# Attention with softmax exponentials shared by ScalarE and VectorE: five shifted readings instead of six, key tiles shared out by the plan, more buffers

## The chip, the cores and the metric

The kernel runs on one core of a Trainium2 chip: TensorE (PE in the profile's rows, its weight loads PEld), VectorE (DVE), ScalarE (ACT), GpSimd (POOL) and SyncE (SP, which issues transfers). The metric is the device time of one execution in microseconds (us), the median of several runs. A traced execution has a span, from its first to its last instruction, and a time of its own a little above it.

## The reference

One transformer block over 2048 tokens of width 512, with 32 heads of 16, conditioned by a vector `c`:

```python
mod = (_silu(c) @ w_mod).reshape(c.shape[0], 6, 1, -1)
h = _layernorm(x) * (1 + ca) + sa
# _A_ref: 32 heads, Dh = 16
scores = jnp.einsum('bhqd,bhkd->bhqk', q, k) * Dh ** (-0.5)
p = _softmax(scores, axis=-1)
o = jnp.einsum('bhqk,bhkd->bhqd', p, v)
x = x + ga * _A_ref(h, A_wqkv, A_wo)
h = _layernorm(x) * (1 + cb) + sb
x = x + gb * _B_ref(h, B_w1, B_b1, B_w2, B_b2)   # 512 -> 1376 -> 512, gelu
```

The exponentials are 32 x 2048 x 2048 = 134 million values, and they carry the time.

## The kernel before

**Runs and tiles.** Queries go in four blocks of 512. A run is one block with four heads at a time; there are 32 runs (0 to 31), eight to a block. (The last block's runs hold eight heads and half the queries.) Within a run the keys go in 16 tiles of 128. A key tile has two halves, each of two heads: one QK matmul pair per half (line 675) writes a PSUM tile `st` of 128x1024 scores, of which there are three.

**Two ways to the exponential.** A tile of ScalarE (kind `qkA`) takes one activation per half (`exp_a`, line 697) into a buffer `pt`, of which there are `NPT` = 7. Then one value matmul group (`pv_op`, line 754, four matmuls) multiplies both halves with the values `VEB` and adds to the run's accumulator `od`. A tile of VectorE (kind `qkD`) takes two additions (`exp_d`, line 712) that turn the scores into 16-bit integers in a buffer `ph` (two of these), whose bits read as bf16 are a piecewise linear exponential. That reading is coarse, so it is averaged with shifted ones: for each further reading j, one VectorE addition of `PH_SH[j]` over 128x2048 integers (line 723) writes a tile `sh`, and one more value matmul group multiplies it with values `VX` that carry a weight `PH_W[j]`. With `NPH` = 6 readings such a tile costs VectorE 2 + 5 instructions and TensorE six value groups. The weighted values `VX` are made once by GpSimd (line 620).

**The accumulator is one PSUM bank.** There is a single `od`. At the end of a run VectorE copies it out (`normalise`, line 782), and only then can the next run's first value group start. Until then the next run's exponentials pile up in `pt`.

**Who takes which tile.** Key tiles 2, 6, 10 and 14 (`DKS`) can go to VectorE. A table `PAT` fixes how many of them do in each run: none in run 0, three in runs 1 to 4, three or four afterwards. The lists `a_list` and `d_list` hold the tiles in order.

**What sets the order.** A planner (`Plan`) simulates the engines with fixed durations while the program is written out. It picks the next instruction of each engine by start time and a priority (`dyn`), and that order is what each engine then runs, in order, on the chip. QK matmuls for VectorE are gated: a run's tile is not begun ahead of ScalarE's run (after run 4, at most one run ahead). All other TensorE work (projections, the output product, the two layers of the feed-forward part, in `block_tail`) carries due times: these count ScalarE exponentials done (`n_a[1]`), with steps such as `APR`, `TAIL` and `CB`. `TAIL` spreads a block's output and feed-forward work over the runs of the next block. Where TensorE would idle, the planner inserts dummy matmuls on `warm` (into `od`, line 760, or `ax`, line 352).

**After the last run,** `last_half` computes the output of the last 256 queries: it needs `od` of run 31 (line 970, a shuffle, then reciprocals at line 979).

Of the kernel before, what the change touches and what calls it, by code (L numbers as in the profile page):

```python
# [16 lines left out]
I16 = mybir.dt.int16  # L17
# [4 lines left out]

NPH = 6
PH_SH = [round(128 * j / NPH) for j in range(NPH)]


# [193 lines left out]
def kernel(  # L222
# [15 lines left out]
    P = 128  # L238
    S = 2048
    D = 512  # L240
    F = 1376
    NC = D // P
    NT = S // P
    QB = 512
# [6 lines left out]
    QSC = 0.25 * 128.0 / math.log(2.0)  # L251
    ESC = math.log(2.0) / 128.0
    DKS = (2, 6, 10, 14)
    NPT = 7
    FEW = 2
    MM = 512 / 2400.0
    PAT = [0] + [3] * 4 + [4] * 3 + [3, 4, 3, 4, 4, 4, 4, 4] * 3

    psum = bass.MemoryType.PSUM
    const = ctx.enter_context(tc.tile_pool(name="const", bufs=1))  # L260
# [7 lines left out]
    def res(name, n, shape, dt, pool=work):  # L268
        return Res(name, n, lambda i: pool.tile(shape, dt, name=f"{name}{i}"))
# [2 lines left out]
    r_od = res("od", 1, [P, QB], FP32, pp)  # L272
    r_ax = res("ax", 1, [P, QB], FP32, pp)
    r_pt = res("pt", NPT, [P, 2 * QB], BF16)
    r_ph = res("ph", 2, [P, 4 * QB], I16)
    r_sh = res("sh", 4, [P, 4 * QB], I16)
    r_xb = res("xb", 2, [P, TPB, D], BF16)
    r_blk = res("blk", NQ, [P, NC, D], BF16)
# [15 lines left out]
    n_a = [0, 0]  # L294
    n_d = [0, 0]
    urgent = set()
    aux_at = [0.0]

    def dyn(plan, o):
        if o.eng != "PE":  # L300
            return o.prio
        same = -0.5 if o.mode[0] == plan.mode else 0.0
        if o.kind == "qkA":
            back = n_a[0] - n_a[1]
            return (0.0 if back == 0 else 2.2 if back == 1 else 6.0) + same
        if o.kind == "qkD":
            back = n_d[0] - n_d[1]
            return (1.0 if back == 0 else 7.0) + same
        if o.kind == "pv":
            few = sum(f <= plan.now + 0.3 for f in r_pt.free) <= FEW  # L310
            return (0.2 if few else 3.0) + same
        if o.kind in urgent:
            return 0.5 + same
        if o.due <= n_a[1]:
            return 2.5 + same
        return (4.0 if plan.now >= aux_at[0] else 8.0) + same

    def later(o):
        return o.kind not in ("qkA", "qkD", "pv", "last", "heat") and o.kind not in urgent and o.due > n_a[1]

    APR = 26
    TAIL, CB = 150, 40
    TAIL2, TAIL3 = 120, 90
    plan = Plan(dyn, later)
    plan.need = lambda: plan.free["ACT"] + 0.92 * (n_a[0] - n_a[1])
    due_now = [1e9, 0.0]
# [8 lines left out]
    def due(at, step=0.0):  # L335
        due_now[:] = [at, step]
# [12 lines left out]
    def heat():  # L349
        if o_warm.end is None or plan.now > plan.until:  # L350
# [29 lines left out]
    VX = {(t, ph): keep.tile([P, 32 * VW + 15], BF16, name=f"VX{t}_{ph}")  # L380
          for t in DKS for ph in range(1, NPH)}
    kT = [[keep.tile([P, QB], BF16, name=f"kT{cc}_{b}") for b in range(NQ)] for cc in range(NC)]
# [212 lines left out]
    def make_v(b, cc, kind, acq, eng):  # L595
# [16 lines left out]
        for t in DKS:  # L612
            if t // TPB == b:
# [4 lines left out]
                def scale(o, t=t, vf=vf):  # L618
                    for ph in range(1, NPH):
                        nc.gpsimd.tensor_scalar(  # L620
# [11 lines left out]
    NR = len(runs)  # L632
    LAST = NQ - 1
# [3 lines left out]
        b, u = runs[r]  # L637
        return (u % NC, None, u // NC) if b == LAST else (u // 2, u % 2, None)

    def dks(r):  # L640
        return DKS[:PAT[r]]
    a_list = []
    d_list = []
    for r in range(NR):
        dk = dks(r)
        a_list += [(r, kt, h) for kt in range(NT) if kt not in dk for h in range(2)]
        d_list += [(r, kt, h) for kt in dk for h in range(2)]
    o_e = {}
    left = [0] * NR
    begun = [False] * NR  # L650
# [1 line left out]
    o_last = [None] * NR  # L652
    o_OT = {}
    a_run = [0]
    made = {"A": 0, "D": 0}
    pv_left = {}

    def qk_op(which, n):
        r, kt, half = (a_list if which == "A" else d_list)[n]
        b = runs[r][0]  # L660
        cc, par, hb = run_heads(r)
        kb, ko = divmod(kt, TPB)
        qm, evs = o_q[(cc, b)]

        def go(o):
            (n_a if which == "A" else n_d)[0] += 1
            q_left[(cc, b)] -= 1
            if q_left[(cc, b)] == 0:
                qm.uses -= 1
            if which == "A":  # L670
                a_run[0] = r
            for g in range(2):
                i = 2 * half + g
                rows = slice(32 * i, 32 * i + 32)
                nc.tensor.matmul(out=o.tile[:, g * QB:(g + 1) * QB],  # L675
                                 lhsT=kT[cc][kb][rows, ko * P:(ko + 1) * P],
                                 rhs=qm.tile[rows, par, :] if hb is None else
                                 qm.tile[rows, :, hb * HB:(hb + 1) * HB], start=True, stop=True)
            nxt(which)
        if which == "D" and half == 0:  # L680
            o_ph[0] = op("POOL", None, 0.0, (), lat=0.0, prio=0.0, acq=r_ph)
        o = op("PE", go, MM, ([o_ph[0]] if which == "D" else []) + [evs[par or 0]] + [o_k[(cc, kb)]], lat=PEL, mode=("qk", half),
               kind="qk" + which, acq=r_st, rel=(qm,),
               gate=(lambda: n_a[0] - n_a[1] < 2) if which == "A" else
               (lambda: n_d[0] - n_d[1] < 2 and r <= a_run[0] + (r > 4)))
        (exp_a if which == "A" else exp_d)(o, r, kt, half)

    def nxt(which):
        made[which] += 1
        todo.append(which)  # L690

    todo = []

    def exp_a(qk, r, kt, half):
        def go(o):
# [77 lines left out]
        plan.add(o)  # L773

    for r in range(NR):
        left[r] = NT + len(dks(r)) * (NPH - 1)
    ended = []


# [112 lines left out]

    def block_tail(b, nt=TPB):
        kind = "tail"
        due(n_a[1] + 12, (TAIL if b < LAST - 1 else TAIL2 if b < LAST else TAIL3) / (9 * nt - 1))
        N = nt * P
        xr = load_x(b)
        x2 = xr
# [3 lines left out]
        for t in range(nt):  # L902
# [11 lines left out]
        h, hd, za, trs = layer_norm(lambda t: x2.tile[:, t, :], res_done, modB, o_late["mB"],  # L914
                                    None, r_blk, ("DVE",) * 4, r_ax, kind, 1.6, None, nt)
# [123 lines left out]
    for b in range(NQ):  # L1039
        kind = f"in{b}"  # L1040
        if b < 2:
            urgent.add(kind)
        o_h[b], o_hd[b], za, trs = layer_norm(
            lambda t, b=b: o_x[b].tile[:, t, :], o_x0 if b == 0 else [o_x[b]] * TPB, modA, o_mA, prev_tr, r_blk,
# [18 lines left out]
    q_made = [0]  # L1063

    def first_run(g):
        return 2 * g if g < LAST * NC else LAST * 8 + g - LAST * NC

    def want_q(g):
        while q_made[0] < g and q_made[0] + 1 < NQ * NC:
            q_made[0] += 1  # L1070
            b, cc = divmod(q_made[0], NC)
            due(32 + APR * (first_run(q_made[0]) - 1) - 26)
            make_q(b, cc, f"q{q_made[0]}", r_ax)
            due(1e9)
            if cc == NC - 1:
                o_h[b].uses -= 1
                if b == NQ - 1:
                    o_w[0].uses -= 1

    state = {"late": 0}  # L1080
    qk_op("A", 0)
    want_q(1)
    qk_op("D", 0)
    while True:
        if not plan.step():
            break
        while todo:
            which = todo.pop(0)
            n = made[which]
            lst = a_list if which == "A" else d_list  # L1090
            if n < len(lst):
                r = lst[n][0]
                want_q(r // 2 + 1 if r < LAST * 8 else r - LAST * 4 + 2)
                qk_op(which, n)
        while ended:
            r = ended.pop(0)
            if r < NR - 1:
                normalise(r)
            b, u = runs[r]
            for cc in range(1, NC):  # L1100
                if r >= 2 * cc - 3:
                    urgent.add(f"c{cc}")
                    urgent.add(f"in{cc}")
            urgent.add("in3")
            for g in range(NQ * NC):
                if first_run(g) <= r + 2:
                    urgent.add(f"q{g}")
            if r == 0:
                late_loads(o_last[0])
                o_late["ga"] = gate_bc(ga_bc, o_late[2], "gate")  # L1110
                lt = {3: o_late[3], 4: o_late[4]}
                gt = o_late["g"]

                class V:
                    pass
                va, vb = V(), V()
                o_late["mB"] = None
                state["gt"] = gt
# [53 lines left out]
```

## Time and profile before

| | us |
|---|---|
| median of 3 runs | 890.87 |
| lowest and highest | 885.26, 892.78 |
| the profiled execution's own time | 886.78 |
| its span | 884.9 |
| POOL busy in the span | 102.5 |

The profiled execution is 4.1 us (0.5%) under the median and 1.9 us above its own span. In the profile's rows, `x` stands for a count, busy time is a union of intervals, and a wait names the instruction that waited, then what released it. A tile's number tells one use of a buffer from another.

### The profile page before, as it was taken

Reading aid. Unit: us, or ns where it says so; the run is one execution under the profiler, and the core shown is the slowest. Engines: PE = TensorE matmul, PEld = TensorE weight load, DVE = VectorE, ACT = ScalarE, POOL = GpSimd, SP = SyncE. Lnnn points to the kernel's source line nnn. Section 1 sums busy time; section 2 is a strip of 40 time slices with the busy share of each in tenths; the row PEclk is TensorE's granted clock in tenths of the full one; section 3 lists DMA queues with packets and bytes.
Section 4 is the critical chain, followed back from the end, with each engine's and each line's share of the span. In section 5 each row is a group of like instructions: output and inputs, shape, how many; then the busy total and the mean of one; then the engine's idle time right before and its main releaser. Section 6 shows DMA issues by size and latency. Waiting matters only on the chain.

```text
span 884.9 us, 20946 instructions
## 1 busy us (share of the span) xinstructions
PE 799.5 (90%) x8725; PEld 305.0 (34%) x8806; DVE 806.6 (91%) x1178; ACT 784.4 (89%) x834; POOL 102.5 (12%) x231
## 2 busy tenths in 40 slices
PE   8889999898899998999998898898889998999887
PEld 3433333332233332232222332232244443444433
DVE  7748889799999999999899999999999998989993
ACT  3799999999899998998899799999989699998752
POOL 4531312200001100000001000000002000000010
PEclk9999999999999999999899999999999998999999
DMA  6204001011000000000100000000100000000000
GB/s 191 96 12 108 14 14 39 14 35 35 32 15 14 14 14 14 21 27 8 37 14 13 14 15 14 8 26 20 37 16 15 16 12 29 26 21 21 10 31 24
DMA packets 31625, 25.13 MB, mean 28 GB/s; under 512 B 13773, under 2 KB 26926, under 8 KB 31530
## 3 DMA queue, kind: packets, MB, share of 16 engines
q1 hardware_dynamic: 31002, 23.78, 9.2%
q8 instruction: 69, 1.13, 0.5%
q14 instruction: 26, 0.21, 0.1%
q10 hardware_dynamic: 528, 0.00, 0.0%
HBM read 21.16 MB, written 2.61 MB: 27 GB/s over the span
## 4 chain that ended last, share of the span: by engine, by line
DVE 40%; PE 27%; ACT 24%; issue 8%; POOL 1%; DMA 0%; POOLq 0%; ACTq 0%; DVEq 0%
DVE ln_s L485 2%; PE od_8878 L754 1%; PE od_12701 L754 1%; PE od_5765 L754 1%; PE od_3837 L754 1%; PE od_12171 L754 1%; ACT g_4820 L928 1%; DVE g_7884 L925 1%; PE od_8082 L754 0%; PE ax_12106 L890 0%; PE od_13281 L754 0%; PE od_9269 L754 0%; DVE OD_14324 L979 0%; PE od_11607 L754 0%; PE od_6173 L754 0%
## 5 line engine op out<-in xcount | busy, mean ns | idle before, releaser
L754 PEld LDWEIGHTS <-VEB_89 128*32 128x32 bf16 x640 | 16.8, 98 | 19.9 <-issue 15.3
L754 PEld LDWEIGHTS <-VEB_91 128*32 128x32 bf16 x640 | 16.8, 96 | 15.7 <-issue 12.7
L754 PEld LDWEIGHTS <-VEB_92 128*32 128x32 bf16 x640 | 16.0, 96 | 14.3 <-issue 11.8
L754 PEld LDWEIGHTS <-VEB_90 128*32 128x32 bf16 x640 | 15.9, 96 | 14.4 <-issue 10.9
L921 PEld LDWEIGHTS <-W_83 128*128 128x128 bf16 x176 | 13.9, 97 | 19.5 <-issue 11.5
L675 PEld LDWEIGHTS <-kT_0_113 32*128 32x128 bf16 x128 | 6.5, 91 | 21.4 <-issue 19.2
L675 PEld LDWEIGHTS <-kT_0_117 32*128 32x128 bf16 x128 | 6.9, 91 | 20.4 <-issue 19.6
L675 PEld LDWEIGHTS <-kT_0_121 32*128 32x128 bf16 x128 | 6.8, 91 | 19.5 <-issue 19.0
L675 PEld LDWEIGHTS <-kT_3_124 32*128 32x128 bf16 x128 | 7.0, 91 | 17.4 <-issue 16.8
L675 PEld LDWEIGHTS <-kT_1_114 32*128 32x128 bf16 x128 | 6.4, 92 | 18.9 <-issue 16.3
L675 PEld LDWEIGHTS <-kT_2_115 32*128 32x128 bf16 x128 | 7.0, 91 | 17.1 <-issue 15.1
L675 PEld LDWEIGHTS <-kT_2_127 32*128 32x128 bf16 x128 | 6.7, 91 | 17.7 <-issue 17.0
L675 PEld LDWEIGHTS <-kT_1_126 32*128 32x128 bf16 x128 | 6.0, 91 | 19.3 <-issue 18.5
L675 PEld LDWEIGHTS <-kT_1_118 32*128 32x128 bf16 x128 | 6.8, 91 | 16.8 <-issue 16.2
L675 PEld LDWEIGHTS <-kT_0_125 32*128 32x128 bf16 x128 | 7.0, 91 | 16.0 <-issue 15.3
L501 ACT ACTIVATE blk_14329<-ax_14416,modB 128x256 bf16<-128x256 bf16 x2 | 1.0, 561 | 13.0 <-PE ax_14416 L1002 13.0
L675 PEld LDWEIGHTS <-kT_1_122 32*128 32x128 bf16 x128 | 5.9, 91 | 18.7 <-issue 18.5
L675 PEld LDWEIGHTS <-kT_3_116 32*128 32x128 bf16 x128 | 6.2, 91 | 17.3 <-issue 15.9
L675 PEld LDWEIGHTS <-kT_2_123 32*128 32x128 bf16 x128 | 6.3, 91 | 16.3 <-issue 15.8
L675 PEld LDWEIGHTS <-kT_2_119 32*128 32x128 bf16 x128 | 6.2, 91 | 16.1 <-issue 15.8
L675 PEld LDWEIGHTS <-kT_3_128 32*128 32x128 bf16 x128 | 5.8, 91 | 17.0 <-issue 16.8
L675 PEld LDWEIGHTS <-kT_3_120 32*128 32x128 bf16 x128 | 5.9, 91 | 16.5 <-issue 15.9
(5047 smaller groups left out, 3274.9 us busy)
## 6 DMA issues: line engine op xcount, KB each, us to landing
W_83<-in_B_w_dram SPq DMA_DIRECT2D x1, 1376.0 KB
g_1026<-in_w_mod_dram SPq DMA_DIRECT2D x2, 512.0 KB
xb_131<-in_A_x_dram SPq DMA_DIRECT2D x4, 128.0 KB
blk_181<-in_w_mod_dram SPq DMA_DIRECT2D x1, 512.0 KB
blk_185<-in_w_mod_dram SPq DMA_DIRECT2D x1, 512.0 KB
w_210<-in_A_wqkv_dram SPq DMA_DIRECT2D x1, 512.0 KB
w_214<-in_A_wqkv_dram SPq DMA_DIRECT2D x1, 512.0 KB
xb_219<-in_A_x_dram SPq DMA_DIRECT2D x1, 512.0 KB
```

Source lines behind the costliest of these rows:

```text
L485: nc.vector.bn_stats(out=st6, in_=src)
L501: nc.scalar.activation(out=dst, in_=src, func=ACT.Identity, bias=mod[:, j:j + 1], scale=mod[:, NC + j:NC + j + 1])
L675: nc.tensor.matmul(out=o.tile[:, g * QB:(g + 1) * QB], lhsT=kT[cc][kb][rows, ko * P:(ko + 1) * P], rhs=qm.tile[rows, par, :] if hb is None ...
L754: nc.tensor.matmul(out=o_od[r].tile[32 * i:32 * i + 32, n * HB:n * HB + w], lhsT=v_tile(kt, ph)[:, c0:c0 + 32], rhs=got[i // 2][:, at:at + ...
L921: nc.tensor.matmul(out=o.tile[:, 0:N], lhsT=W1[:, j, f * P:(f + 1) * P], rhs=h.tile[:, j, 0:N], start=(j == 0), stop=(j == NC - 1))
L925: ev.append(op("DVE", lambda o, f=f, mm=mm: nc.vector.tensor_scalar(out=g.tile[:, f, 0:N], in0=mm.tile[:, 0:N], scalar1=b1c[:, f:f + 1], s ...
L928: ge = op("ACT", lambda o: nc.scalar.activation(out=g.tile[:, :, 0:N], in_=g.tile[:, :, 0:N], func=ACT.Gelu_apprx_tanh), 0.1 + 1.2 * nt + ...
```

## The change

Five readings instead of six (`NPH`); three `ph` buffers instead of two; nine `pt` buffers instead of seven. The table `PAT` is gone. ScalarE owns the tiles outside `DKS` (and all of run 0); tiles in `DKS` are shared, and each engine asks `next_tile` for work when its last QK matmul has been placed. VectorE takes the first shared tile of the run that `d_run` names: a run ahead of ScalarE's, or ScalarE's own, where at least 6 us (`D_TIME`) of ScalarE work are left in it by the plan. ScalarE takes a shared tile when a run's own tiles are used up. VectorE's next tile is placed when a `ph` buffer is free within 1 us of the plan's time and the run is ScalarE's or (after run 3) the next. Due times count both engines' halves, 32 a run, with the steps raised in proportion.

```diff
-NPH = 6
+NPH = 5
...
-    NPT = 7
+    NPT = 9
...
-    PAT = [0] + [3] * 4 + [4] * 3 + [3, 4, 3, 4, 4, 4, 4, 4] * 3
+    FIRST_D, D_TIME = 1, 6.0
...
-    r_ph = res("ph", 2, [P, 4 * QB], I16)
+    r_ph = res("ph", 3, [P, 4 * QB], I16)
...
-        if o.due <= n_a[1]:
+        if o.due <= n_a[1] + n_d[1]:
...
-    APR = 26
-    TAIL, CB = 150, 40
-    TAIL2, TAIL3 = 120, 90
+    APR = 32
+    TAIL, CB = 185, 49
+    TAIL2, TAIL3 = 148, 110
...
+    own = [[kt for kt in range(NT) if r < FIRST_D or kt not in DKS] for r in range(NR)]
+    shared = [[kt for kt in DKS if r >= FIRST_D] for r in range(NR)]
+    at = {"A": [0, 0, 1], "D": [0, 0, 1]}
...
+    def d_run():
+        for r in range(max(at["D"][0], a_run[0]), NR):
+            if shared[r] and (r > a_run[0] or D_TIME < 0.92 * (
+                    2 * (len(own[r]) + len(shared[r]) - 1) + n_a[0] - n_a[1])):
+                return r
+        return NR
...
+            if which == "A" and own[r]:
+                return r, own[r].pop(0), 0
+            if which == "A" and shared[r]:
+                left[r] -= NPH - 1
+                return r, shared[r].pop(), 0
+            if which == "D" and shared[r] and r >= d_run():
+                return r, shared[r].pop(0), 0
...
-               (lambda: n_d[0] - n_d[1] < 2 and r <= a_run[0] + (r > 4)))
+               (lambda: n_d[0] - n_d[1] < 2))
...
-        due(n_a[1] + 12, (TAIL if b < LAST - 1 else TAIL2 if b < LAST else TAIL3) / (9 * nt - 1))
+        due(n_a[1] + n_d[1] + 15, (TAIL if b < LAST - 1 else TAIL2 if b < LAST else TAIL3) / (9 * nt - 1))
...
+        if not live["A"]:
+            qk_op("A")
+        if not live["D"] and (at["D"][2] == 0 or (min(r_ph.free) <= plan.now + 1.0
+                                                  and d_run() <= a_run[0] + (a_run[0] > 3))):
+            qk_op("D")
```

Counted over the two programs' instructions:

| engine, kind | before | after |
|---|---|---|
| DVE scores to integers (712 before, 733 after) | 228 | 246 |
| DVE shifts (723, 744) | 570 | 492 |
| ACT exponentials (697, 718) | 796 | 778 |
| PE value matmuls on `sh` | 2880 | 2480 |
| PE value matmuls on `pt` and `ph` | 2560 | 2560 |
| PE dummy matmuls into `od` (760, 781) | 156 | 176 |
| POOL values `VX` weighted, and their memsets | 80, 40 | 64, 32 |
| SP | 168 | 168 |

So VectorE takes 123 tiles instead of 114, of 124 that may be shared: runs 1 to 4 have four instead of three, run 5 has three, every later run four.

VectorE at the end of run 25, where block 2's output and feed-forward work (`blk`, `g`) runs between the attention of block 3. `od_10524` is run 25's accumulator before; `sh` rows are shifts, `ph` of two numbers are two tiles. Before:

```order
L723 TENSOR_SCALAR sh_11029<-ph_10795 128x2048
L712 TENSOR_SCALAR ph_10983<-st_11021 128x1024
L504 TENSOR_SCALAR blk_10663<-ax_11031,modB 128x512
L723 TENSOR_SCALAR sh_11059<-ph_10795 128x2048
L723 TENSOR_SCALAR sh_11066<-ph_10795 128x2048
L504 TENSOR_SCALAR blk_10663<-ax_11061,modB 128x512
L723 TENSOR_SCALAR sh_11089<-ph_10795 128x2048
L723 TENSOR_SCALAR sh_11097<-ph_10983 128x2048
L586 TENSOR_TENSOR qm_10271<-ax_11091,qmask 128x1024
L782 COPY OD_11112<-od_10524 128x512
```

The run's last tile (`ph_10795`) still has four shifts to go, and a shift of the next tile and a query mask stand before the copy. After, the same place, with `od_10186` the accumulator:

```order
L744 TENSOR_SCALAR sh_10686<-ph_10328 128x2048
L733 TENSOR_SCALAR ph_10643<-st_10683 128x1024
L504 TENSOR_SCALAR blk_10356<-ax_10688,modB 128x512
L744 TENSOR_SCALAR sh_10716<-ph_10328 128x2048
L744 TENSOR_SCALAR sh_10723<-ph_10328 128x2048
L504 TENSOR_SCALAR blk_10356<-ax_10718,modB 128x512
L744 TENSOR_SCALAR sh_10750<-ph_10500 128x2048
L803 COPY OD_10758<-od_10186 128x512
```

The last tile has three shifts there, the query mask has gone ahead, and the integers of two later tiles (`ph_10500`, `ph_10643`) are already made.

VectorE at the end of run 31, the last. Before, in front of the shuffle that starts the last stage:

```order
L723 TENSOR_SCALAR sh_14224<-ph_14005 128x2048
L925 TENSOR_SCALAR g_13501<-ax_14219,b1c 128x256
L723 TENSOR_SCALAR sh_14251<-ph_14005 128x2048
L723 TENSOR_SCALAR sh_14253<-ph_14147 128x2048
L723 TENSOR_SCALAR sh_14263<-ph_14147 128x2048
L723 TENSOR_SCALAR sh_14273<-ph_14147 128x2048
L723 TENSOR_SCALAR sh_14288<-ph_14147 128x2048
L925 TENSOR_SCALAR g_13501<-ax_14283,b1c 128x256
L723 TENSOR_SCALAR sh_14307<-ph_14147 128x2048
L925 TENSOR_SCALAR g_13501<-ax_14309,b1c 128x256
```

All these come behind the last exponential's scores, and the run's last value group is that of `sh_14307`. After:

```order
L744 TENSOR_SCALAR sh_13616<-ph_13427 128x2048
L744 TENSOR_SCALAR sh_13626<-ph_13427 128x2048
L744 TENSOR_SCALAR sh_13644<-ph_13427 128x2048
L744 TENSOR_SCALAR sh_13659<-ph_13427 128x2048
L946 TENSOR_SCALAR g_13067<-ax_13692,b1c 128x256
L946 TENSOR_SCALAR g_13067<-ax_13724,b1c 128x256
```

The last shift now stands ahead of the last scores, and the run's last value group is that of ScalarE's last tile.

More of the change, by code (lines that the diff above doesn't have):

```diff
@@ L318, in later @@
     def later(o):
-        return o.kind not in ("qkA", "qkD", "pv", "last", "heat") and o.kind not in urgent and o.due > n_a[1]
-    APR = 26
-    TAIL, CB = 150, 40
-    TAIL2, TAIL3 = 120, 90
+        return o.kind not in ("qkA", "qkD", "pv", "last", "heat") and o.kind not in urgent and o.due > n_a[1] + n_d[1]
+    APR = 32
+    TAIL, CB = 185, 49
+    TAIL2, TAIL3 = 148, 110
     plan = Plan(dyn, later)
@@ L638, in run_heads @@
         return (u % NC, None, u // NC) if b == LAST else (u // 2, u % 2, None)
[L640 to L647, printed above, removed]
+    own = [[kt for kt in range(NT) if r < FIRST_D or kt not in DKS] for r in range(NR)]
+    shared = [[kt for kt in DKS if r >= FIRST_D] for r in range(NR)]
+    at = {"A": [0, 0, 1], "D": [0, 0, 1]}
     o_e = {}
@@ L654, with next_tile, qk_op @@
     a_run = [0]
-    made = {"A": 0, "D": 0}
     pv_left = {}
-    def qk_op(which, n):
-        r, kt, half = (a_list if which == "A" else d_list)[n]
+    def d_run():
[4 more added lines that the diff above has]
+        return NR
+    def next_tile(which):
+        r, kt, half = at[which]
+        if half == 0:
+            return r, kt, 1
+        while r < NR:
+            if which == "A" and own[r]:
[5 more added lines that the diff above has]
+                return r, shared[r].pop(0), 0
+            r += 1
+        return None
+    def qk_op(which):
+        got = next_tile(which)
+        if got is None:
+            return
+        at[which][:] = got
+        r, kt, half = got
+        want_q(r // 2 + 1 if r < LAST * 8 else r - LAST * 4 + 2)
+        live[which] += 1
         b = runs[r][0]
@@ L678, in go @@
                                  qm.tile[rows, :, hb * HB:(hb + 1) * HB], start=True, stop=True)
-            nxt(which)
+            live[which] -= 1
         if which == "D" and half == 0:
@@ L684, in qk_op @@
                gate=(lambda: n_a[0] - n_a[1] < 2) if which == "A" else
-               (lambda: n_d[0] - n_d[1] < 2 and r <= a_run[0] + (r > 4)))
+               (lambda: n_d[0] - n_d[1] < 2))
         (exp_a if which == "A" else exp_d)(o, r, kt, half)
[L688 to L692, printed above, removed]
+    live = {"A": 0, "D": 0}
     def exp_a(qk, r, kt, half):
@@ L775 @@
     for r in range(NR):
-        left[r] = NT + len(dks(r)) * (NPH - 1)
+        left[r] = NT + len(shared[r]) * (NPH - 1)
     ended = []
@@ L1071, in want_q @@
             b, cc = divmod(q_made[0], NC)
-            due(32 + APR * (first_run(q_made[0]) - 1) - 26)
+            due(32 + APR * (first_run(q_made[0]) - 1) - 32)
             make_q(b, cc, f"q{q_made[0]}", r_ax)
@@ L1080 @@
     state = {"late": 0}
-    qk_op("A", 0)
+    qk_op("A")
     want_q(1)
-    qk_op("D", 0)
     while True:
+        if not live["A"]:
+            qk_op("A")
+        if not live["D"] and (at["D"][2] == 0 or (min(r_ph.free) <= plan.now + 1.0
+                                                  and d_run() <= a_run[0] + (a_run[0] > 3))):
+            qk_op("D")
         if not plan.step():
             break
[L1087 to L1094, printed above, removed]
         while ended:
```

## The prediction

> **What bounds the kernel now.** I read the busy shares first, then the same by stage, then what each engine waited for, and last the end of the chain. The profile's first part:
>
> ```profile
> span 884.9 us, 20946 instructions
> PE 799.5 (90%) x8725; PEld 305.0 (34%) x8806; DVE 806.6 (91%) x1178; ACT 784.4 (89%) x834; POOL 102.5 (12%) x231
> ```
>
> Three engines are at 90%, so no single one carries the time. By stage (the stretch's length, then busy time of each engine, then the granted clock):
>
> ```profile
> 75.00:200.00 125.00, 115.28 (x1179) 42.87 (x1189) 107.61 (x160) 121.99 (x133) 23.65 (x41) 0.97 0.10 28
> 200.00:850.00 650.00, 593.21 (x6822) 220.54 (x6883) 626.78 (x880) 600.25 (x628) 44.84 (x39) 0.98 0.07 19
> 75.00:850.00 775.00, 708.48 (x7997) 263.41 (x8072) 734.38 (x1039) 722.24 (x759) 68.49 (x80) 0.98 0.07 21
> ```
>
> From 75 to 850 us runs 1 to 31 go on; DVE is busy 734.4 of 775 us (94.8%), ACT 722.2 (93.2%), PE 708.5 (91.4%). From 200 us on DVE is at 96.4%: it is the fullest, and ACT has 49.8 us idle there. What ends ACT's idle time in that stretch, longest first:
>
> ```profile
> ACT pt_11151 L697 <- PE od_11122 L754: 6.3, 1, 6.3
> ACT pt_7743 L697 <- PE od_7730 L754: 5.1, 1, 5.1
> ACT pt_13883 L697 <- PE od_13854 L754: 4.8, 1, 4.8
> ACT pt_13314 L697 <- PE od_13281 L754: 4.2, 1, 4.2
> ACT pt_3854 L697 <- PE od_3837 L754: 2.8, 1, 2.8
> ACT pt_6580 L697 <- PE od_6563 L754: 2.5, 1, 2.5
> ACT pt_6954 L697 <- PE od_6941 L754: 2.4, 1, 2.4
> ACT pt_10081 L697 <- PE od_10051 L754: 2.4, 1, 2.4
> ACT pt_8500 L697 <- PE od_8487 L754: 2.0, 1, 2.0
> ACT pt_5387 L697 <- PE od_5374 L754: 1.8, 1, 1.8
> ...
> ACT pt_2254 L697 <- PE st_2245 L675: 1.1, 1, 1.1
> ```
>
> Ten waits make 34.3 us of ACT's 52.8 us idle. Each is for a value matmul into a new accumulator, that is, the end of a run. The longest, in order of time on ACT and DVE:
>
> ```profile
> 690.54 1.04 ACT L697 ACTIVATE pt_11050<-st_11047 128x1024 bf16<-128x1024 f32 x1
> 697.88 1.02 ACT L697 ACTIVATE pt_11151<-st_11053 128x1024 bf16<-128x1024 f32 x1 [6.30 <-PE od_11122 L754]
> ...
> 692.67 0.70 DVE L723 TENSOR_SCALAR sh_11089<-ph_10795 128x2048 int16<-128x2048 int16 x1
> ...
> 696.06 0.68 DVE L782 COPY OD_11112<-od_10524 128x512 f32<-128x512 f32 x1
> ```
>
> DVE is late with the last shift of run 25 (693.4 us); the accumulator is copied at 696.1, the next run's first value matmul follows, frees a `pt` buffer, and ACT goes on at 697.9. All seven `pt` buffers held exponentials of run 26 until then. So I counted, in the program's order before, how many of the next run's ScalarE scores stand on PE ahead of a run's last value group. It is seven or more (as many as there are buffers) at the ends of runs 7, 11, 14, 15, 17, 19, 23, 25, 29 and 30, and these are exactly the ten waits above; at all other ends it is six or fewer. That is the rule I use below.
>
> **The change, part by part.** Durations are from these sums over a line (busy time, count) and the table loads among the first:
>
> ```profile
> 0.00:890.00 890.00, 746.84 (x799) 0.98 0.10 28
> ...
> 0.00:890.00 890.00, 278.06 (x228) 0.98 0.10 28
> ...
> 0.00:890.00 890.00, 377.87 (x570) 0.98 0.10 28
> ...
> 0.00:890.00 890.00, 341.65 (x5440) 126.27 (x5440) 0.98 0.10 28
> ...
> L697 ACT ACT_TABLE_LOAD x3 | 3.8, 1283 | 0.1
> ```
>
> In this order they are the exponentials (line 697), the integers (712), the shifts (723) and the value matmuls (754). An exponential is (746.8 - 3.8) / 796 = 0.933 us, an integer half 278.06 / 228 = 1.220, a shift 377.87 / 570 = 0.663, a value matmul 341.65 / 5440 = 0.063.
>
> *VectorE.* A tile costs 2 x 1.220 + 5 x 0.663 = 5.75 us before and 5.09 with four shifts. 114 x 5.75 = 655.9 becomes 123 x 5.09 = 626.2: 29.7 us less, or 734.4 - 29.7 = 704.7 us from 75 us on. Runs 1 to 5 get 19 tiles instead of 16, so DVE gains 4.7 us of work there, where it has 17.4 idle; the relief, 34.4 us, is all in runs 6 to 31.
>
> *ScalarE.* Nine tiles fewer are 18 exponentials: 18 x 0.933 = 16.8 us off an engine that is on the path at both ends of every run. This comes off the end: **-16.8**.
>
> *TensorE.* 400 value matmuls fewer x 0.063 = 25 us; 20 dummies more give some 2 back. PE's 708.5 goes to about 685. It is not the fullest engine before or after, so this is counted at nothing; the work of ACT and DVE covers it. Were PE the bound instead, its 23 us would come off in place of the terms here, and the time would be 864.
>
> *The run ends.* Two more `pt` buffers let ACT run two exponentials further, and the shorter tail of shifts, with integers made up to three tiles ahead, brings the copy earlier. By the same count, now against nine buffers, nine or more stand ahead only at the ends of runs 4 and 25 (eleven each), 10 and 18 (nine each); elsewhere it is eight or fewer. Four waits of the present mean, 34.3 / 10 = 3.4 us, instead of ten: **-20.6**. The bounds are 0 (every end waits as long as now for another reason) and -34.3 (none waits). I take the count, since it named all ten of the present waits and no other.
>
> *The last run.* Its end before:
>
> ```profile
> 847.71 1.03 ACT L697 ACTIVATE pt_14217<-st_14198 128x1024 bf16<-128x1024 f32 x1
> ...
> 852.73 0.68 DVE L723 TENSOR_SCALAR sh_14307<-ph_14147 128x2048 int16<-128x2048 int16 x1
> ...
> 853.47 0.40 PE L754 MATMUL od_13854<-sh_14307,VX_5_112 128*32 128x256 bf16 x8
> ...
> 854.02 0.74 DVE L970 STREAM_SHUFFLE OD_14324<-od_13854 128x512 f32<-128x512 f32 x1
> ```
>
> The last stage starts 6.3 us behind the last exponential, since DVE still shifts. After, the last shift stands ahead of the last scores, so the shuffle follows an exponential (1.0), a value group (0.4) and the step to DVE (0.1 to 0.8): about 2.3 us. **-4.0**, between 0 and -4.4.
>
> *What is given back.* These three would leave 775 - 16.8 - 20.6 = 737.6 us for 704.7 us of DVE work, 95.5% against 94.8% now. A queue that waits less for one partner waits for another, so I hold DVE to the share that it has now over the whole stretch: 704.7 / 0.948 = 743.3, **+5.7**. The bounds are 0 and, if nothing of the run ends is gained, +20.6.
>
> *At nothing.* `VX` weights and memsets on GpSimd (24 instructions fewer, engine 12% busy, early); the buffers' memory; SP's queue, which is not moved. Due times go from 24 to 26 halves a run to 32, and the steps with them (`TAIL` 150 to 185), so the projections and the feed-forward part stay where they were within a fifth of a run.
>
> **Sum.** -16.8 - 20.6 - 4.0 + 5.7 = -35.7 against the profiled execution's 886.8: **851**. That execution lies 4.1 us under the median of its runs, so a median may come out some us higher.
>
> **The rivals.**
>
> *Only ScalarE's own work goes.* The run ends wait as long as before, now for DVE's backlog of integers made ahead. For it: DVE is the fullest engine, and three `ph` buffers let later tiles' integers stand in front of a run's last shifts. Against it: in the order of run 25's end one such shift stands before the copy, as now. 886.8 - 16.8 = **870**.
>
> *All run ends are cured.* The st waits alone remain (about 1 us each), and DVE packs as it does now from 200 us on: 704.7 / 0.964 = 731, so 775 - 731 = 44 us less and 4 at the end: **839**. Against it: at run 25's end the order still has ACT filling all its buffers.
>
> *The clock.* PE loses work, and its clock follows:
>
> ```profile
> core 0: 884.9 us, clock 0.983
> ...
> 431.00:446.00 15.00, 14.08 (x113) 3.97 (x110) 12.68 (x19) 11.67 (x14) 0.00 (x0) 0.77 0.01 3
> ```
>
> The granted clock averages 0.983, so 15 us of full clock are lost over the span, in spells; in the one at 431 to 446 us ACT and DVE are both below their mean. If PE, with 23 us less work, lost twice as much, and each us of it reached the end, that gives 15 us back: **866**. For it: the planner itself puts in 20 more dummies. Against it: PE has 66 us idle to take this up, and the dummies are there to hold the clock. The Trainium skill, "TensorE: Matmul & The Clock Gate", Part 1, says that a TensorE which is idle for about one window (3.4 us) falls to half clock; by that rule work taken off PE can slow what is left. The trace agrees that the clock falls in spells in a kernel whose PE is 90% busy; which gap starts one it does not show.
>
> *Slower.* The planner takes VectorE to be faster than it is: its durations (1.14 and 0.6 us) make a new tile 4.68 us, the trace's 5.09, so four tiles are 1.6 us late a run. If the new sharing had used up the slack that absorbs this, each of 31 run ends would wait, and by more than now: to end slower by over 1% it takes 35.7 + 8.9 = 44.6 us, 1.4 us at each end beyond the forecast: **896**. The place is PE, where scores for VectorE that wait for a PSUM tile hold up ScalarE's behind them:
>
> ```profile
> PE st_12054 L675 <- DVE ph_12029 L712: 0.7, 1, 0.7
> ...
> DVE ph_6913 L712 <- PE st_6975 L675: 2.0, 1, 2.0
> ```
>
> Against it: the longest such wait is 0.7 us, DVE waits longer for scores than scores for DVE, and the same lateness (0.47 us a tile before) is in the trace already.
>
> *Not what it says.* "By which has time" is nearly a fixed table again: 123 of 124 shared tiles go to VectorE. That changes no number above, since the counts are the order's.
>
> **How the numbers follow.** Chances: the forecast 0.56, only ScalarE's own 0.16, all run ends cured 0.11, the clock 0.08, planner's lateness 0.09, of which 0.05 ends within 1% and 0.04 slower. Within 1%, 8.9 us, is about what a measurement of this kernel can tell from no change. Range: from the cured case, 838, to ScalarE's alone, 871. Faster 0.56 + 0.16 + 0.11 + 0.08 = 0.91, same 0.05, slower 0.04.
>
> **What would show it.** Right: about 765 to 768 us of ACT busy time and 777 of DVE; `od` waits of ACT over 1.5 us only at the ends of runs 4, 10, 18 and 25; the shuffle within 3 us of the last exponential; DVE near 95% from 75 us to the last run's end. Wrong: a wait of ACT on `od` at many run ends (first rival), a mean clock under 0.97 (third), or waits of PE for `ph` that sum to more than 10 us (fourth). A DVE share under 93% with ACT under 93% as well would mean that something else, PE's order, bounds the runs.

## The result, and the profile after

The changed kernel takes 842.37 us (median of 4 runs, 840.82 to 851.38) against 888.07 for the kernel before beside it: a ratio of 0.951, with a 95% interval of 0.942 to 0.960. It is faster by about 5%. A ratio here and below leaves out the few runs that were over 1.5% longer than the fastest of their kernel, at a lower granted clock. The profiled execution takes 842.59 us, its span is 840.8.

The profile's first part after, busy time and share of the span for each engine:

```profile
span 840.8 us, 20060 instructions
PE 768.7 (91%) x8345; PEld 292.4 (35%) x8424; DVE 775.4 (92%) x1118; ACT 768.3 (91%) x816; POOL 97.6 (12%) x207
```

All three engines have less work and all three are a little fuller. The stretch from 75 us to the last exponential, with the busy time of PE, PEld, DVE, ACT and POOL, and then the granted clock:

```profile
75.00:806.00 731.00, 678.19 (x7657) 251.70 (x7727) 706.94 (x982) 703.18 (x739) 66.80 (x73) 0.99 0.08 22
```

DVE is busy for 96.7% of it (94.8% before), ACT for 96.2% (93.2%). What ended ACT's idle time there, longest first:

```profile
ACT pt_10808 L718 <- PE od_10763 L775: 4.1, 1, 4.1
ACT pt_12923 L718 <- PE od_12824 L775: 2.7, 1, 2.7
ACT pt_2710 L718 <- PE od_2695 L775: 2.5, 1, 2.5
ACT pt_11310 L718 <- PE od_11264 L775: 1.9, 1, 1.9
ACT pt_7899 L718 <- PE od_7872 L775: 1.5, 1, 1.5
ACT pt_4929 L718 <- PE od_4903 L775: 1.5, 1, 1.5
ACT pt_6019 L718 <- PE st_6010 L700: 1.1, 1, 1.1
```

In order these are the ends of runs 25, 29, 4, 26, 18 and 10; before, six such waits were 2.5 us and longer. All waits for a new accumulator sum to 16.2 us, where they were 38.3; all waits for scores (`st`) to 10.1, where they were 12.7.

The sums over the lines of the exponentials (718), the integers (733), the shifts (744) and the value matmuls (775), in this order:

```profile
0.00:890.00 890.00, 730.67 (x781) 0.99 0.10 28
...
0.00:890.00 890.00, 299.16 (x246) 0.99 0.10 28
...
0.00:890.00 890.00, 324.54 (x492) 0.99 0.10 28
...
0.00:890.00 890.00, 315.19 (x5040) 114.70 (x5040) 0.99 0.10 28
```

Exponentials cost 16.2 us less (746.8 before), the two VectorE lines 32.2 us less together, value matmuls 26.5 us less. The end of the last run, in order of time:

```profile
803.58 0.68 DVE L744 TENSOR_SCALAR sh_13659<-ph_13427 128x2048 int16<-128x2048 int16 x1
...
806.65 1.07 ACT L718 ACTIVATE pt_13729<-st_13711 128x1024 bf16<-128x1024 f32 x1
...
808.80 0.73 DVE L991 STREAM_SHUFFLE OD_13747<-od_13299 128x512 f32<-128x512 f32 x1
```

The shuffle comes 2.15 us behind the start of the last exponential (6.31 before). What follows it takes 32.0 us to the end of the span, 1.1 more than before. So the span's 44.1 us add up along ScalarE: 16.2 of exponentials, 22.1 of accumulator waits, 4.2 at the last run, 2.6 of score waits, less 1.1 at the end, are 44.0. Such a sum says where the time went, not what took it away; the experiments are about that.

### The profile page after: what moved, and what is told of

Its sections match the earlier page's. It is cut to its first block, busy times and chain, and to the rows that moved or that the text cites. A ratio compares the mean times of both kernels' runs of the same rounds, so it can differ in the third digit from the quotient of the medians.

```text
span 840.8 us, 20060 instructions
## 1 busy us (share of the span) xinstructions
PE 768.7 (91%) x8345; PEld 292.4 (35%) x8424; DVE 775.4 (92%) x1118; ACT 768.3 (91%) x816; POOL 97.6 (12%) x207
## 4 chain that ended last, share of the span: by engine, by line
PE 31%; DVE 30%; ACT 30%; issue 8%; DMA 0%; POOL 0%; DVEq 0%; ACTq 0%
DVE ln_s L485 1%; PE od_8586 L775 1%; PE od_5655 L775 1%; PE od_13299 L775 1%; ACT g_7608 L949 1%; PE ax_13807 L911 1%; PE od_2171 L775 1%; PE od_5986 L775 1%; PE od_4903 L775 1%; PE od_10763 L775 0%; DVE g_4655 L946 0%; PE od_9703 L775 0%; PE od_1024 L775 0%; DVE OD_13747 L1000 0%; PE od_7494 L775 0%
## 5 line engine op out<-in xcount | busy, mean ns | idle before, releaser
L775 PEld LDWEIGHTS <-VEB_89 128*32 128x32 bf16 x640 | 16.8, 97 | 15.5 <-issue 11.2
L700 PEld LDWEIGHTS <-kT_0_121 32*128 32x128 bf16 x128 | 8.0, 91 | 22.2 <-issue 21.7
L700 PEld LDWEIGHTS <-kT_0_109 32*128 32x128 bf16 x128 | 7.4, 91 | 20.2 <-issue 17.5
L700 PEld LDWEIGHTS <-kT_2_111 32*128 32x128 bf16 x128 | 7.4, 91 | 19.3 <-issue 17.4
L700 PEld LDWEIGHTS <-kT_0_113 32*128 32x128 bf16 x128 | 7.1, 91 | 19.7 <-issue 19.0
L700 PEld LDWEIGHTS <-kT_1_122 32*128 32x128 bf16 x128 | 7.1, 91 | 18.7 <-issue 18.4
L700 PEld LDWEIGHTS <-kT_1_110 32*128 32x128 bf16 x128 | 6.7, 91 | 18.7 <-issue 16.6
L700 PEld LDWEIGHTS <-kT_2_123 32*128 32x128 bf16 x128 | 7.8, 91 | 15.4 <-issue 14.8
L700 PEld LDWEIGHTS <-kT_0_117 32*128 32x128 bf16 x128 | 6.9, 91 | 17.8 <-issue 17.4
L700 PEld LDWEIGHTS <-kT_2_115 32*128 32x128 bf16 x128 | 6.8, 91 | 17.3 <-issue 16.6
L700 PEld LDWEIGHTS <-kT_3_124 32*128 32x128 bf16 x128 | 7.1, 91 | 16.1 <-issue 15.9
L700 PEld LDWEIGHTS <-kT_3_120 32*128 32x128 bf16 x128 | 6.8, 91 | 17.2 <-issue 16.6
L700 PEld LDWEIGHTS <-kT_2_119 32*128 32x128 bf16 x128 | 6.3, 91 | 18.0 <-issue 18.0
L700 PEld LDWEIGHTS <-kT_1_118 32*128 32x128 bf16 x128 | 6.6, 91 | 17.1 <-issue 16.1
L700 PEld LDWEIGHTS <-kT_3_116 32*128 32x128 bf16 x128 | 6.9, 91 | 16.2 <-issue 15.4
L700 PEld LDWEIGHTS <-kT_3_112 32*128 32x128 bf16 x128 | 6.5, 91 | 17.2 <-issue 15.8
L700 PEld LDWEIGHTS <-kT_1_114 32*128 32x128 bf16 x128 | 6.2, 91 | 17.7 <-issue 17.1
```

The source lines that it names most:

```text
L700: nc.tensor.matmul(out=o.tile[:, g * QB:(g + 1) * QB], lhsT=kT[cc][kb][rows, ko * P:(ko + 1) * P], rhs=qm.tile[rows, par, :] if hb is None ...
L775: nc.tensor.matmul(out=o_od[r].tile[32 * i:32 * i + 32, n * HB:n * HB + w], lhsT=v_tile(kt, ph)[:, c0:c0 + 32], rhs=got[i // 2][:, at:at + ...
```

## The experiments

Each ratio is against the kernel before in runs on the same chip, with its 95% interval. Two theories stood against each other at first. The *run-end theory* is the prediction's: ScalarE's work plus its waits for the accumulator. The *VectorE theory* says that VectorE's work at a fixed share sets the time.

### 1. Five readings only

```diff
-NPH = 6
+NPH = 5
```

in the kernel before: the same table of tiles, the same buffers, the same 796 exponentials.

> The kernel before with five readings, all else as before: table of tiles, seven pt buffers, two ph buffers, 796 exponentials. Run-end theory (ScalarE's work plus its waits for the accumulator at run ends): same ScalarE work; in the new order no run end has seven or more of the next run's scores ahead, so the 34 us of long waits go; four shifts instead of eight stand behind the last scores, 2 us: 888 - 36 = 852. VectorE theory (the time follows VectorE's work at a fixed share): 114 shifts x 0.663 = 76 us less work, at 95% 80 us: about 809.

Measured: 844.85 us, 0.954 (0.949 to 0.959). The waits of ACT from 75 us to the last exponential, summed by kind (sum, times, longest), and the busy times there:

```profile
ACT pt L697 <- PE st L675: 10.9, 26, 2.0
ACT pt L697 <- PE od L754: 1.8, 2, 1.6
...
75.00:807.00 732.00, 671.06 (x7456) 250.11 (x7514) 670.75 (x923) 718.28 (x758) 63.00 (x73) 0.99 0.08 22
```

The accumulator waits are gone (38.3 to 1.8 us), ScalarE is busy for 98.1%, and VectorE, with 75 us less work (377.9 to 303.1 us of shifts), has fallen to 91.6%. The waits went as the run-end theory said, and the VectorE theory is out by 36 us. The line also takes 576 value matmuls off TensorE (5440 to 4864, 34 us less busy time), and this run doesn't separate that from the shorter tail of shifts. This one line carries nearly all of the change's gain by itself (0.954 against 0.951).

### 2. Buffers only

```diff
-    NPT = 7
+    NPT = 9
...
-    r_ph = res("ph", 2, [P, 4 * QB], I16)
+    r_ph = res("ph", 3, [P, 4 * QB], I16)
```

in the kernel before.

> The kernel before with nine pt and three ph buffers, six readings and the table kept. Run-end theory: ScalarE work the same; nine or more scores ahead at six ends instead of seven or more at ten, so 4 x 3.4 = 14 us less, and twelve shifts instead of eight behind the last scores, 2 us more: about 876. VectorE theory: its work is the same, so 888.

Measured: 892.86 us, 1.009 (1.005 to 1.014): no gain. The loss of about 1% may be the clock alone (last section). ACT's waits by kind, and the busy times:

```profile
ACT pt L697 <- PE od L754: 28.9, 10, 8.6
ACT pt L697 <- PE st L675: 17.0, 38, 1.4
...
75.00:844.00 769.00, 701.91 (x7976) 262.68 (x8053) 736.91 (x1035) 721.33 (x759) 71.72 (x80) 0.98 0.08 21
```

There are ten accumulator waits, the longest is 8.6 us, and VectorE is at 95.8%. The tail of shifts is no shorter: the shuffle at the last run comes 7.3 us behind the start of the last exponential, where it came 6.3 behind. That ScalarE runs further ahead and then waits longer at one place fits with this, but single run ends were not followed. My count (nine or more ahead at six ends, 20 us) missed the size, and the gain did not come.

### 3. Sharing only

The changed kernel with six readings and the old buffers:

```diff
-NPH = 5
+NPH = 6
...
-    NPT = 9
+    NPT = 7
...
-    r_ph = res("ph", 3, [P, 4 * QB], I16)
+    r_ph = res("ph", 2, [P, 4 * QB], I16)
```

> The changed kernel's sharing by the plan and its due times, with six readings, seven pt and two ph buffers as before. The plan gives VectorE 109 tiles instead of 114. Run-end theory: ten exponentials more, +9.3 us; seven or more ahead at five ends instead of ten, -17; no shift behind the last scores, -4: about 876. VectorE theory: 5 tiles x 5.75 = 29 us less, at 95% 30: about 858.

Measured: 871.49 us, 0.981 (0.972 to 0.989). The run-end theory's 876 is nearer than 858. The accumulator waits are 7.7 us in five. The plan gives VectorE five tiles fewer, and ten exponentials more use up part of what the waits save.

### 4. The old table's tiles in the changed kernel

```diff
-    own = [[kt for kt in range(NT) if r < FIRST_D or kt not in DKS] for r in range(NR)]
-    shared = [[kt for kt in DKS if r >= FIRST_D] for r in range(NR)]
+    PAT = [0] + [3] * 4 + [4] * 3 + [3, 4, 3, 4, 4, 4, 4, 4] * 3
+    own = [[kt for kt in range(NT) if kt not in DKS[:PAT[r]]] for r in range(NR)]
+    shared = [list(DKS[:PAT[r]]) for r in range(NR)]
```

> The changed kernel, but only as many tiles of a run may be shared as the old table gave VectorE: 114 tiles and 796 exponentials, with five readings and the new buffers. Run-end theory: against before no ScalarE work saved, no end with nine ahead, -34, nothing behind the last scores, -4: about 850, so that against the changed kernel the 18 exponentials (+17) are nearly paid by the waits that go (-16). VectorE theory: 9 tiles x 5.09 = 46 us less than in the changed kernel: under 800.

Measured: 850.91 us, 0.959 (0.952 to 0.966). The run-end theory's 850 holds, the VectorE theory's 800 does not. The nine tiles that the changed kernel moves to VectorE buy about 1% by these ratios, 0.959 and 0.951, and their intervals overlap, so it may be nothing.

### 5 to 8. The same extra work on one engine, before and after

An instruction that the plan does not know of, in unchanged order, at one place in each of runs 1 to 31. On VectorE:

```diff
+                if j == 1 and kt == 6:
+                    nc.vector.tensor_scalar(out=spare, in0=first.tile, scalar1=PH_SH[j],
+                                            scalar2=None, op0=ALU.add)
```

and on ScalarE:

```diff
+            if kt == 8 and half == 0 and r > 0:
+                nc.scalar.activation(out=spare, in_=qk.tile, func=ACT.Exp, scale=ESC)
```

> The kernel before, in unchanged order, with one more shift (written to a spare tile that nobody reads) behind the first shift of key tile 6 in runs 1 to 31: 31 x 0.66 = 20.6 us more VectorE work. If VectorE's work sets the time before: +18 to +21 us. If ScalarE's work plus run-end waits set it: only the ten ends that wait get later by 0.66 each, +7 us.

> The kernel before, in unchanged order, with one more exponential (written to a spare tile that nobody reads) behind the first half of key tile 8 in runs 1 to 31: 31 x 0.90 = 28 us more ScalarE work. If VectorE's work sets the time before, ScalarE's 50 us of idle time take most of it: under +10 us. If ScalarE's work plus run-end waits set it: ten ends hide it in their wait, the others don't, +19 us or more.

> The changed kernel, in unchanged order, with the same extra shift in runs 1 to 31: 20.6 us more VectorE work. If VectorE still sets the time: +18 us or more. If ScalarE's work plus run-end waits set it now: +3 to +7 us. If both are equally full: about +10.

> The changed kernel, in unchanged order, with the same extra exponential in runs 1 to 31: 28 us more ScalarE work. If ScalarE sets the time now: +25 us or more. If VectorE still sets it: under +10. If both are equally full: about +15.

Measured, with the changed kernel's 0.951 taken off for the last two:

| extra work | in the kernel before | in the changed kernel |
|---|---|---|
| VectorE, 20.6 us | 1.017 (1.012 to 1.023): +15 us | 0.975 (0.970 to 0.980): +21 us |
| ScalarE, 28 us | 1.025 (1.021 to 1.030): +22 us | 0.986 (0.979 to 0.992): +31 us |

Each us is worked out as the difference of ratios times 884; the changed kernel's own ratio is uncertain by 0.009, so its two figures are by 8 us. Neither theory gave both lines. Each named one engine whose work counts and one that has room; in both kernels work added to either comes out at the end, three quarters of it before and about all of it after. Part of that is a lower clock in these runs (a median of 0.976 to 0.981, against 0.986 in both kernels without the work). Read at the same clock, as the last section does, it is +13 and +18 us before, +17 and +22 after: about two thirds, then four fifths. The rows of the changed kernel with the extra exponential, what TensorE waited for and what VectorE waited for (sum, times, longest):

```profile
PE st L701 <- ACT pt L719: 28.4, 93, 0.5
PE st L701 <- ACT spare L721: 17.7, 28, 0.9
...
DVE ph L736 <- PE st L701: 27.8, 42, 2.4
```

TensorE waits for the extra exponential 28 times, up to 0.9 us, since it holds its PSUM tile longer. The scores behind that in TensorE's order come late for VectorE too: it waits 27.8 us for scores, where it waited 12.3 (19 waits, the longest 1.8). With the extra shift it goes the other way round: TensorE's waits for shifts go from 5.4 to 13.3 us, and ScalarE's waits for scores from 10.1 to 18.8. So each added instruction does two things, it takes time of its engine and it keeps a buffer that others need, and no run here has the one without the other.

### 9. Extra work on TensorE

```diff
+            if kt == 8 and ph == 0 and r > 0 and not first:
+                for i in range(12):
+                    nc.tensor.matmul(out=o_od[r].tile[32 * (i % 4):32 * (i % 4) + 32, :],
+                                     lhsT=warm[:, 0:32],
+                                     rhs=warm[:, 0:1].to_broadcast([P, QB]), start=False,
+                                     stop=False, tile_position=(0, 32 * (i % 4)))
```

> The changed kernel, in unchanged order, with twelve more dummy matmuls into the accumulator behind the value group of key tile 8 in runs 1 to 31: 372 x 0.063 = 23 us more TensorE work. If the engines move in step through TensorE's queue, so that work added to any of them comes out at the end: +15 to +23 us. If TensorE's 50 us of idle time take it: 0 to +5 us, or a little less than nothing by a higher clock.

Measured: 859.3 us, 0.973 (0.969 to 0.977), that is +20 us of the 23 expected (the rows have 25.6 us busy for the 372 matmuls). TensorE is no exception. ACT's waits by kind:

```profile
ACT pt L718 <- PE st L700: 22.4, 57, 1.0
ACT pt L718 <- PE od L775: 18.5, 10, 5.3
```

It waits 22.4 us for scores instead of 10.1. A third theory fits experiments 5 to 9 better than either: the three engines go in step, tied by the order of TensorE's work and by three PSUM tiles, so that work added to any of them at a place that the plan did not foresee shows in large part at the end. It is argued from the waits. No run had more PSUM tiles or another order of the same work, so the tie itself is not shown, and neither is it shown for work that is taken off.

### 10. More dummies

```diff
-HEAT = 1.3
+HEAT = 1.5
```

> The changed kernel with the planner's constant for keeping TensorE busy (HEAT) at 1.5 instead of 1.3: 412 dummy matmuls into the accumulator instead of 176, 780 exponentials. If the lost clock costs about 6 us for each hundredth (the slope over single runs so far) and the dummies fill idle time: clock 0.995 and about 837. If dummies are TensorE work that comes out at the end: 236 x 0.063 = 15 us more, about 857 less what the clock gives, 852.

Measured: 860.05 us, 0.973 (0.970 to 0.975). The granted clock does rise:

```profile
core 0: 858.7 us, clock 0.994
```

but the kernel is 2% slower than the changed one. The dummies into the accumulator are TensorE work like that of experiment 9. The plan also changed with them (accumulator waits of 28.3 us, where they were 16.2), so the two can't be told apart here.

### 11. Seven buffers in the changed kernel

```diff
-    NPT = 9
+    NPT = 7
```

> The changed kernel with seven pt buffers instead of nine; the plan gives VectorE all 124 tiles, 776 exponentials. Run-end theory with the count of scores ahead: seven or more at seven ends, 24 us of long waits instead of the 16 measured with nine buffers: about 850. If the buffers only move the wait from one place to another, as the run with buffers alone suggests: 840 to 843.

Measured: 856.48 us, 0.970 (0.966 to 0.974). ACT's waits by kind:

```profile
ACT pt L718 <- PE od L775: 26.4, 15, 6.0
ACT pt L718 <- PE st L700: 11.0, 33, 0.9
```

The count gave 24 us of accumulator waits, measured are 26.4, ten more than with nine buffers. With six readings, two more `pt` buffers and one more `ph` were worth nothing; the two `pt` buffers are worth 2% here, where the plan loads VectorE with four tiles in nearly every run. About half of the 2% may be the clock (a median of 0.978 against 0.986): at the same clock 8 us are left, near to the ten of the waits.

### 12. Four readings

```diff
-NPH = 5
+NPH = 4
```

in the changed kernel; the approximation of the exponential gets coarser.

> The changed kernel with four readings: three shifts a tile, 123 x 0.663 = 82 us less VectorE work, 778 exponentials as in the changed kernel (the approximation of the exponential is coarser). If ScalarE is then the floor, as in the run with five readings only, where it was busy 98% from 75 us to the last exponential: 704 / 0.98 = 718 instead of 731 us, about 829. If every us of VectorE still comes off the end: 770 to 780.

Measured: 845.08 us, 0.957 (0.952 to 0.963): nothing gained over five in these times. The stretch to the last exponential, what VectorE waited for, and the clock:

```profile
75.00:817.00 742.00, 683.06 (x7215) 243.74 (x7216) 646.05 (x862) 708.64 (x742) 57.64 (x66) 0.96 0.08 21
...
DVE ph L733 <- PE st L700: 42.5, 46, 4.4
...
core 0: 851.2 us, clock 0.960
```

VectorE is busy for 61 us less than in the changed kernel and idle for 72 us more; the largest part of that is waiting for scores (42.5 us against 12.3). ScalarE is at 95.5%, not at the 98% that I expected, and the granted clock has fallen to 0.960 in this execution and to 0.960 to 0.980 over four. The clock hides something: at the same clock, four readings lie 7 us under the changed kernel (last section), still far from the 770 to 780 us that stood for VectorE's work alone. In the times as measured, no version here beats the changed kernel.

## Why the prediction was right, and where it was off

The time, 842.4 against 851 in a range of 838 to 871, was faster as forecast, by 5% where I had 4%. The terms of the sum came out nearly as written, except one; the causes that I gave for them did so only in part.

- *ScalarE, -16.8:* right as a term, -16.2 by the lines' sums, but not as a gain of its own. With the 18 exponentials back on ScalarE (experiment 4) the time rises by about 1% (7 us, with intervals that overlap), not by 16, and with five readings alone ScalarE has all 796 of them and the time is nearly the same. The nine tiles bring run-end waits with them that use up most of what they save; the sum had this trade in it, but as two separate gains.
- *The run ends, -20.6:* right in size, -22.1. The four ends that the count named are among the six longest waits (4.1, 2.5, 1.5, 1.5 us), but their mean is 2.4 us instead of 3.4, and ends with eight ahead (29 and 26) wait 2.7 and 1.9. So the size is in part luck: smaller waits at more places. Before, too, the count named the ten longest, but not all: five shorter ones (0.4 to 1.3 us, 4.0 together) stand at ends with fewer scores ahead. What I gave as the cause was two things together, more buffers and a shorter tail of shifts. Experiments 1 and 2 part them: five readings alone take the waits from 38.3 to 1.8 us, the buffers alone leave ten of them and gain no time. The buffers matter only behind that: with seven `pt` buffers the plan gives VectorE even one tile more, 124, and 26.4 us of accumulator waits stand where nine buffers leave 16.2 (experiment 11).
- *The last run, -4.0:* right, -4.2.
- *What is given back, +5.7:* this is the term that was off. I held VectorE to its share of 94.8% and gave as the reason that a queue that waits less for one partner waits for another. It went to 96.7%, and ScalarE's waits for scores fell too (12.7 to 10.1). Integers placed up to three tiles ahead fit with that, but no run tested them by themselves. Without this term the sum gives 845, against the profiled 842.6.
- *TensorE at nothing:* the number came out, the reason did not. I took it that the work of ACT and DVE covers TensorE's, with 66 us of its time idle. Experiment 9 shows that in the changed kernel some 20 us of added work of 23 to 26 come out at the end. Since 400 matmuls were taken away here, TensorE may have a part in the gain that my sum put down to run ends; the experiments don't separate it, because no version took work off TensorE alone.
- *The rivals.* The one that all run ends are cured (839) came nearest in the number: it has VectorE at 96.4% and a stretch of 731 us, and the profile has 96.7% and 731. Its condition did not come, since 16.2 us of accumulator waits are left. So I had the run ends right, and that rival had VectorE's share right. ScalarE alone (870) fell: the waits went. The clock (866) fell for this change: it is 0.986 in the profiled execution, 0.983 before. It is not ruled out as a mechanism: in experiment 12, with VectorE's and TensorE's work cut further, the clock was lower. The slower rival fell: the longest wait of TensorE for an integer is 0.7 us, and those waits sum to 4.3 us over the stretch, where they were 7.5.
- *The signs.* ACT's 768.3 us and DVE's 775.4 of busy time and the shuffle's 2.15 us came as written. DVE near 95% did not, and accumulator waits over 1.5 us stand at the ends of runs 25, 29, 4 and 26, not at 4, 10, 18 and 25.

One reading of the prediction was incomplete. At the end of run 25 before, ACT stood still from 691.6 to 697.9 us, and I put that down to VectorE's last shift, which ended at 693.4. Most of the wait comes behind that shift. The clock over the first half of the wait, then TensorE and VectorE in it:

```profile
691.20:694.60 3.40, 3.16 (x27) 1.54 (x27) 2.76 (x5) 0.38 (x1) 0.00 (x0) 0.50 0.00 0
...
693.99 0.90 PE L573 MATMUL ax_11091<-blk_637,w_214 128*128 128x512 bf16 x2 [0.22 <-issue]
694.82 0.40 PE L754 MATMUL od_10524<-sh_11089,VX_5_112 128*32 128x256 bf16 x8
...
694.92 1.23 DVE L586 TENSOR_TENSOR qm_10271<-ax_11091,qmask 128x1024 bf16<-128x1024 f32 x1 [0.96 <-PE ax_11091 L573]
```

The last shift's value group stands behind a projection that runs mostly at half the clock, and VectorE waits for that same projection to make the query mask, which stands ahead of the copy. So the order of other work, and the clock, had a part in the longest of the ten waits.

## What to carry to other kernels

Where three engines are each 90% busy and wait for each other, as here, ask of every edit how much work it takes off each of them, and don't book an engine's last few per cent of idle time as room: extra work on any of three engines came out at the end at about three quarters or more, and at two thirds to four fifths when read at the same clock. Here more buffers were worth nothing while VectorE was late, and 1 to 2% once its work was cut. When a wait has an engine's name on it, cut that engine's work first and look where the next wait appears: with five readings ScalarE itself was busy 98%, and in the changed kernel a further cut of VectorE (four readings) left the time where it was. Before calling a change of 1% a gain or a loss, set the clocks of the two kernels side by side.

## What the runs showed of the hardware

The spread between runs of one kernel goes with the granted clock. In 27 runs of the kernel before, beside the experiments, the time goes from 890.6 us at a clock of 0.973 to 877.1 at 0.998; a straight line through them has a slope of 5.4 us for a hundredth of the clock and leaves 1.2 us. The other kernels' lines have 4.4 to 7.2. So of the 8.9 us of clock that a hundredth is, about 60% reach the end. The medians of two kernels whose clocks differ by a hundredth are therefore about 5 us apart for that alone. The kernel with the buffers alone had a median clock of 0.966 against 0.985 beside it, worth 10 us on that line, so its 7.5 us may be nothing else. This is read from the runs; no experiment set the clock by itself.

So I read every kernel also at the same clock, as the mean distance of its runs from one of these lines. The changed kernel's own line rests on four runs (6.9 us for a hundredth), not taken beside those of the experiments, so a few us in its column are not certain.

| kernel | from the line of the kernel before, us | from the line of the changed kernel, us |
|---|---|---|
| changed | -40 | |
| five readings only (1) | -36 | +5 |
| buffers only (2) | -2 | |
| sharing only (3) | -15 | |
| the old table's tiles (4) | -37 | +3 |
| before, more VectorE, ScalarE work (5, 6) | +13, +18 | |
| changed, more VectorE, ScalarE, TensorE work (7, 8, 9) | | +17, +22, +18 |
| more dummies (10) | | +22 |
| seven buffers (11) | | +8 |
| four readings (12) | | -7 |

Of the change's 44 us some 40 are thus left at the same clock. Five readings alone give the 36 us that the run-end theory forecast for them.

The clock falls to half in spells of 3.4 or 6.8 us, and not only behind time that counts as idle. In the profiled execution before there are four of the short and two of the long kind from 75 us to the last exponential. Three of them start 0.3 to 1.7 us ahead of one of ACT's ten long waits and overlap it (2.5, 2.4 and 6.3 us, at the ends of runs 14, 15 and 25). A stretch ahead of one of these spells and the spell itself:

```profile
431.50:434.90 3.40, 3.05 (x24) 0.88 (x24) 3.40 (x5) 3.19 (x4) 0.00 (x0) 1.00 0.00 0
434.90:441.70 6.80, 6.25 (x43) 1.73 (x42) 5.02 (x7) 3.90 (x5) 0.00 (x0) 0.52 0.02 4
```

PE counts as busy for 3.05 of the 3.4 us before the clock goes to half. The Trainium skill ("TensorE: Matmul & The Clock Gate", Part 1) has the half clock behind a window of idle time; the lengths of the spells, 3.4 and 6.8 us, agree with one and two of its windows of about 3.4 us, but the busy share of 90% ahead of this one does not look like idle time, and what starts a spell stays open here.
